# Pre-LN attention and SwiGLU block on one core: another order of the softmax round, one score tile copied out by ACT, a cast moved to GpSimd, and a layer norm moved

## The chip, the core and the metric

One core of a Trainium2 chip runs the whole block in one launch. The metric is the device time in microseconds (us), lower is better. The kernel before ran three times: 1196.97, 1195.42 and 1194.06 us, median 1195.42. Engines are called PE (TensorE; PEld is its weight load), DVE (VectorE), ACT (ScalarE), POOL (GpSimd) and SP (SyncE, which here only issues DMAs).

## The reference

```python
S, D, H, Dh, F = 2048, 448, 16, 28, 1792        # one sequence, float32
n = layernorm(x)                                 # no weights, eps 1e-5
q = (n @ wq)  in 16 heads of 28;  k = n @ wk;  v = n @ wv     # one key/value head for all
p = softmax(q k^T * 28**-0.5);  o = p v
h = x + concat(o) @ wo
m = layernorm(h)
out = h + (silu(m @ w1) * (m @ w3)) @ w2
```

## The kernel before

All operands are split into a high and a low part in a rounded format (`fp32r`), and a product takes three matmuls (high by high, low by high, high by low). There are three parts: a start (layer norm, projections, some score maxima), a long softmax loop, and the feed-forward.

**The work of the loop.** Queries lie in 4 tiles `t` of 512, heads in 4 groups `g` of 4; a pair is a *query group* `i = 4t + g`, 16 in all. The 2048 keys lie in 16 chunks `c` of 128. A *step* is one query group on one key chunk; there are 256. The four heads of a group use four row groups of PE, 32 rows each, side by side. The pieces are:

- **Head** (`H0` to `H3`, class `Head`): three matmuls give 128 keys by 512 queries of one head in a PSUM bank (`pb`, L355); after the third ACT takes the exponential into a `pt`, `xh` or `xl` tile (L362). Of the 32 rows of the query tile `qs`, 28 hold the query; rows 28 and 29 hold minus the row maximum, high and low part, against ones in the keys.
- **Value visit** (`pv1`, function `pv`): four products of the exponentials with the values, in a 128-row mode of PE (`po`, L371, eight instructions). After chunk 15 ACT copies the result to `OT` (L378).
- **Maxima**, which must be there before a group's first head: a *unit* is 128 queries by 512 keys of one head (`pa`, L266). `U` is one matmul and a DVE maximum out of PSUM (L276). `D` and `S` deal with two units: `D` multiplies by a difference of keys (`KD`) and ACT keeps the positive part (`ab`, L287), `S` adds the other product to it and takes the maximum on DVE (L294). The code also has `E`, a unit whose scores ACT copies to SBUF (`kept`), and `R`, the DVE maximum of such a copy later; before, no entry of the order uses them.
- **End of a group's maxima**: when its 64 units are counted, `max_done` reduces them (`nm`, DVE) and splits them (`neg`, POOL, two instructions); 20 entries of the order later (`ROWS = 20`) `max_rows` transposes (`mr`, DVE) and `max_out` issues eight DMAs from SP that write rows 28 and 29 of `qs`. The first head matmul of the group waits for all eight.

**The order.** `EVERY` is a list of entries, written out, that is repeated; one pass is a *round* of four value visits, 48 head matmuls and 16 units. Every engine runs its instructions in this order. PSUM has seven banks for scores: a matmul that starts a bank waits until ACT or DVE has read what stood there. Units run 20 steps (`AHEAD`) ahead of the values. Before, the entries between visits hold 13 or 14 matmuls three times and 24 once; that is the *long visit* below.

**Work hung on steps** (`at(step, ...)`): `build_qs(i)` casts a group's queries to the high part on ACT (L247) and makes the low part on POOL; at the end of tile `t` the output projection `wo_rows` (44 matmuls, L163) runs, then statistics, `ln_rstd` and, for tile 0, `ln_norm` (ACT, L208), the first norm of the feed-forward.

Of the kernel before, what the change touches and what calls it, by code (L numbers as in the profile page):

```python
# [10 lines left out]
AF = mybir.ActivationFunctionType  # L11
# [13 lines left out]
NQ = T // P  # L25
NG = H // 4
NC = S // P
# [8 lines left out]
def block_kernel(  # L36
# [13 lines left out]
    ve, se, ge, pe, sy = nc.vector, nc.scalar, nc.gpsimd, nc.tensor, nc.sync  # L50
# [4 lines left out]
    def f(ap):  # L55
        return ap.bitcast(F32)
# [16 lines left out]
    QR = [keep.tile([P, NG, T], F32, name=f"QR{t}") for t in range(NT)]  # L73
# [10 lines left out]
    def qs_tile():  # L84
        k, n_qs[0] = homes[n_qs[0] % len(homes)], n_qs[0] + 1
        return keep.tile([P, 2, T], F32R, name="qs", tag=f"q{k}")
# [56 lines left out]
    def bank(name="pb"):  # L143
        k = min(free, key=lambda k: order[k])
        free.remove(k)
        ps = ps_w.tile([P, T], F32, name=name, tag=f"bank{k}")
        used[id(ps)] = ps, k
        ready.pop(id(ps), None)
        return ps

    def done(ps, at=None):
        k = used.pop(id(ps))[1]
        order[k] = ready.get(id(ps), clock.end) + 0.7 if at is None else at
        free.append(k)
# [61 lines left out]
    def xt_tiles():  # L216
        return [xt_pool.tile([P, m, T], F32R, name=name) for m, name in ((4, "xh"), (3, "xl"))]

    def ln_tr(t, c, spare=False):
        ps = last = bank()  # L220
        if c == 0:
            XT[t] = xt_tiles()
        xh, xl = XT[t]
        xns = LN[t][3]
        for n in range(NQ):
            pe.transpose(ps[:, n * P : (n + 1) * P], xns[n][:, c * P : (c + 1) * P], ident)  # L226
            clock.mm("full", 0, ps, 0.109, n == 0)
        se.activation(xh[:, c], ps, AF.Copy)
        eng = ve
        if spare:  # L230
            x32 = wk_pool.tile([P, T], F32, name="rb")
            se.activation(x32, ps, AF.Copy)
            eng, ps = ge, x32
        if c < 3:
            eng.tensor_tensor(xl[:, c], ps, f(xh[:, c]), op=ALU.subtract)
        else:
            eng.tensor_tensor(xh[64:128, 3], ps[64:128], f(xh[64:128, 3]), op=ALU.subtract)
        done(last)
# [4 lines left out]
    def build_qs(i, ps=None):  # L243
        t, g = divmod(i, NG)
        q = QS[i] = qs_tile()
        if ps is None:
            se.activation(q[:, 0], QR[t][:, g], AF.Copy)  # L247
            ge.tensor_tensor(q[:, 1], QR[t][:, g], f(q[:, 0]), op=ALU.subtract)
        else:
            se.activation(q[:, 0], ps, AF.Copy)  # L250
            ve.tensor_tensor(q[:, 1], ps, f(q[:, 0]), op=ALU.subtract)
# [205 lines left out]
    with tc.tile_pool(name="start", bufs=1) as sp:  # L457
# [76 lines left out]
        def q(t, g, nb=0):  # L534
            ps = bank()
            mm_D(ps, ps, [w[:, :, 4 * g : 4 * g + 4].rearrange("p c h r -> p c (h r)") for w in WQ],
                 XT[t], slice(0, P), slice(0, T), lambda: pairs(nb))
            if t == g == 0:
                build_qs(0, ps)
            else:  # L540
                se.activation(QR[t][:, g], ps, AF.Copy)
            done(ps)
# [56 lines left out]
        q(0, 1, 0)  # L599
        v0 = kv(0, 1)  # L600
        build_qs(1)
        norm(1, False, 1)
        norm(1, False, 3)
# [105 lines left out]
        q(3, 3, 3)  # L709
        pairs(2)  # L710
        build_qs(2)
        q(2, 1, 0)
        pairs(2)
# [33 lines left out]
    def at(s, fn, *args):  # L747
        todo.setdefault(s, []).append((fn, args))
# [6 lines left out]
    for i in range(NI - 1):  # L755
        e = NC * (i + 1)
# [3 lines left out]
    for t in range(NT - 1):  # L760
        e = NC * NG * (t + 1)


        for n in range(NQ):
            at(e + 14.7, wo_rows, t, n)
            if t == 2:
                at(e + 14.7, lambda c: ln_tr(0, c, True), n)
            late = NC * NG * (t + 2) + 14 if t < 2 else LAST - 12
            at(e + 14.7 if n < NQ - 1 else late + 0.7, ln_stats, t, n)
        at(late + 2, ln_rstd, t)  # L770
    for n in range(NQ):
        at(2 * NC * NG + 25 + 2 * n, ln_norm, 0, n, True)
    for t in range(NT - 1):
        for k in range(2):
            at(NC * NG * (t + 1) + 13 + k, load_w13, 2 * t + k)
# [10 lines left out]
    for s in range(AHEAD, LAST):  # L786
        i, c = divmod(s, NC)
        n, kt = divmod(c, NQ)
# [66 lines left out]
        return True  # L855

    LAG = 1
    EVERY = "U1 U0 pv1 D1 H2 U3 H0 H1 H2 H0 H1 H2 U3 H0 H1 U2 pv1 D0 H1 H3 U2 H3 H3 U2 H2 H1 H1 H2 H2 H0 S1 H3 H0 H1 H0 H3 H1 H3 U2 H1 S0 pv1 U0 H3 H2 H1 H0 H3 H1 H2 H0 H3 H2 U1 H0 U3 pv1 U3 H1 H0 H2 H3 H0 H2 H3 H0 H2 H3".split()

    def tick():  # L860
        for x in later:
            x[0] -= 1
        if later and later[0][0] <= 0:
            i = later.pop(0)[1]
            max_rows(i)
            max_out(i)

    ROWS = 20
    while n_pv[0] + LAG < TAIL:
        for x in EVERY:  # L870
            tick()
# [156 lines left out]
```

## Time and profile before

| | |
|---|---|
| median of three runs | 1195.42 us (1194.06 to 1196.97) |
| the profiled execution's own time | 1193.55 us |
| its span, first to last instruction | 1191.8 us |
| PE / DVE / ACT / POOL busy | 99% / 66% / 61% / 28% |
| first value visit, last value visit | at 92.8 us, at 754.6 us |
| granted PE clock, mean | 1.000 |

The loop is more than half of the span. Inside it DVE and ACT are each busy about nine tenths, in the feed-forward after it they are mostly idle and PE sets the pace. A busy PE in this profile includes matmuls whose ends are modelled, so the loop is read by the distance from one value visit to the next and by what each bank waits for.

### The profile page before, as it was taken

What the parts mean: (1) busy time and instruction counts of PE and PEld (TensorE: products, weight loads), DVE (VectorE), ACT (ScalarE), POOL (GpSimd) and SP (SyncE); (2) the same over time, 40 slices, a digit from 0 to 9 for tenths busy, and PEclk for the clock granted to TensorE, in tenths of its full rate; (3) what the DMA queues carried; (4) which work ended last, traced back from release to release, by engine and by line L of the source; (5) the groups of instructions that cost most, each with busy time, mean ns of one, the idle gap of its engine ahead of it and who ended that gap; (6) DMA issues with size and microseconds to landing.
All of it is one profiled execution on the core that took longest, in us unless ns stands there. A gap on an engine that the chain in (4) does not pass through costs nothing.

```text
span 1191.8 us, 22197 instructions
## 1 busy us (share of the span) xinstructions
PE 1174.8 (99%) x8588; PEld 743.4 (62%) x8588; DVE 786.2 (66%) x1474; ACT 729.6 (61%) x1392; POOL 335.9 (28%) x289
## 2 busy tenths in 40 slices
PE   6999999999999999999999999999999999999998
PEld 4664444445444445444446443688888888888887
DVE  7879899887889988889897981354343334333332
ACT  5739999996999996999997999412111111211111
POOL 5312001101010120011022012354555445455552
PEclk9999999999999999999999999999999999999999
DMA  4000000001000001000001000233000000000000
GB/s 163 10 17 21 19 26 18 19 15 45 19 18 4 19 23 38 19 19 11 10 23 46 10 19 19 57 107 86 1 32 1 1 1 31 1 1 32 1 1 32
DMA packets 36618, 30.72 MB, mean 26 GB/s; under 512 B 13216, under 2 KB 31392, under 8 KB 36512
## 3 DMA queue, kind: packets, MB, share of 16 engines
q1 hardware_dynamic: 36512, 29.30, 8.6%
q8 instruction: 67, 1.10, 0.4%
q14 instruction: 39, 0.32, 0.1%
HBM read 20.37 MB, written 3.80 MB: 20 GB/s over the span
## 4 chain that ended last, share of the span: by engine, by line
PE 93%; DVE 3%; ACT 2%; DMA 0%; SPq 0%; issue 0%; POOLq 0%
PE pa L163 27%; PE po L371 20%; PE pb L355 16%; PE pa L266 14%; PE pb L935 11%; PE pb L163 4%; DVE mx L276 2%; PE pb L226 1%; ACT OT L378 1%; ACT ab L287 1%; DMA X<-in_A_x_dram 0%; ACT pt L362 0%; DVE X L939 0%; DVE xn L210 0%; SPq L174 0%
## 5 line engine op out<-in xcount | busy, mean ns | idle before, releaser
L276 DVE TENSOR_REDUCE mx<-pa 128x1 f32<-128x512 f32 x748 | 481.2, 685 | 62.3 <-PE pa L266 49.2
L355 PE MATMUL pb<-qs,KS 32*128 32x512 f32 x3072 | 393.8, 427 | 0.0
L362 ACT ACTIVATE pt<-pb 128x512 f32<-128x512 f32 x684 | 360.0, 618 | 31.0 <-PE pb L355 15.9
L266 PE MATMUL pa<-KS,qs 32*128 32x512 f32 x886 | 332.2, 460 | 1.9 <-ACT ab L287 0.4
L355 PEld LDWEIGHTS pb<-qs,KS 32*128 32x128 f32 x3072 | 228.6, 182 | 45.6 <-issue 12.6
L163 PE MATMUL pa<-xh,qs 128*128 128x512 f32 x896 | 231.2, 390 | 0.0
L266 PEld LDWEIGHTS pa<-KS,qs 32*128 32x128 f32 x886 | 145.2, 182 | 121.1 <-DVE mx L276 96.5
L163 PEld LDWEIGHTS pa<-xh,qs 128*128 128x128 f32 x896 | 168.1, 188 | 33.7 <-issue 0.8
L371 PE MATMUL po<-pt,VA 128*32 128x512 f32 x1368 | 182.2, 604 | 0.0
L923 DVE TENSOR_TENSOR pt<-pa,pt 128x512 f32<-128x512 f32 x56 | 38.7, 691 | 206.7 <-PE pa L163 202.2
L921 ACT ACTIVATE pt<-pa 128x512 f32<-128x512 f32 x56 | 33.5, 599 | 194.1 <-PE pa L163 194.1
L935 PE MATMUL pb<-w2s,pt 128*128 128x448 f32 x660 | 144.7, 368 | 0.2 <-POOL w2s L444 0.2
L935 PEld LDWEIGHTS pb<-w2s,pt 128*128 128x128 f32 x660 | 123.1, 188 | 13.1 <-POOL w2s L444 0.6
L926 ACT ACTIVATE pt<-pt 128x512 fp32r<-128x512 f32 x56 | 35.5, 633 | 153.4 <-DVE pt L923 149.1
L362 ACT ACTIVATE xh<-pb 128x512 f32<-128x512 f32 x170 | 100.8, 622 | 11.1 <-PE pb L355 9.2
L362 ACT ACTIVATE xl<-pb 128x512 f32<-128x512 f32 x170 | 100.4, 618 | 10.0 <-PE pb L355 6.6
L294 DVE CUSTOM_DVE_ANT_0 ab<-pa,ab 128x512 f32<-128x512 f32 x138 | 93.1, 683 | 7.8 <-ACT ab L287 3.9
L163 PE MATMUL pa<-xl,qs 128*128 128x512 f32 x336 | 94.8, 390 | 0.0
L371 PE MATMUL po<-xl,VA 128*32 128x512 f32 x340 | 89.5, 605 | 0.0
L371 PE MATMUL po<-xh,VA 128*32 128x512 f32 x340 | 89.4, 605 | 0.0
L266 PEld LDWEIGHTS pa<-KD,qs 32*128 32x128 f32 x138 | 23.2, 181 | 99.7 <-ACT pt L362 63.7
L287 ACT ACTIVATE ab<-pa 128x512 f32<-128x512 f32 x138 | 81.6, 602 | 5.4 <-PE pa L266 4.5
(102 smaller groups left out, 1021.2 us busy)
## 6 DMA issues: line engine op xcount, KB each, us to landing
rb<-sd SPq DMA_DIRECT2D x64, 64.0 KB
QR<-OT SPq DMA_DIRECT2D x60, 56.0 KB
QR<-in_B_w_dram SPq DMA_DIRECT2D x16, 192.0 KB
X<-in_A_x_dram SPq DMA_DIRECT2D x3, 896.0 KB
out_dram<-X SPq DMA_DIRECT2D x3, 896.0 KB
qs<-mr SPq DMA_DIRECT2D x128, 2.0 KB
w<-in_B_w_dram SPq DMA_DIRECT2D x8, 192.0 KB
w_wo<-in_B_w_dram SPq DMA_DIRECT2D x6, 224.0 KB
```

The source lines that it names most:

```text
L163: pe.matmul(ps, lhs[b][:, cb, lsl], rhs[a][:, ca, rsl], start=(k == 0), stop=(k == len(terms) - 1),)
L266: pe.matmul(ps, QS[i][r, 0, n * P : (n + 1) * P], KS[0][r, kt * T : (kt + 1) * T] if keys is None else keys[r], start=True, stop=True)
L276: ve.tensor_reduce(self.to(), ps, axis=AX.X, op=ALU.max)
L287: se.activation(self.ab, ps, AF.Relu)
L294: ve.tensor_tensor_reduce(self.ab, ps, self.ab, 1.0, -3.0e38, ALU.add, ALU.max, self.to())
L355: pe.matmul(self.ps, KS[k % 2][r, c * P : (c + 1) * P], QS[i][r, k // 2], start=(k == 0), stop=(k == 2))
L362: se.activation(f(PT[i, c, p][:, jj]), self.ps, AF.Exp, bias=0.0, scale=SCALE)
L371: pe.matmul(PO[i][32 * j : 32 * j + 32], VA[:, c], f(PT[i, c, j // 2][:, j % 2]), start=(c == 0), stop=(c == NC - 1))
L921: se.activation(sg, ps[0], AF.Silu)
L923: ve.tensor_tensor(sg, ps[1], sg, op=ALU.mult)
L926: se.activation(h[:, 0], sg, AF.Copy)
L935: pe.matmul(Y[t][n][:, :D], hid[a][:, n * P : (n + 1) * P], w2s[:, b, :D], start=(k == 0 and m == 0), stop=(k == NF - 1 and m == 2))
```

## The change

1. `EVERY` is another list. It still has four value visits, 48 head matmuls and 16 units, but 11 `U`, two `D` with two `S`, and one unit as `E` (ACT copies it to SBUF) with its maximum `R` on DVE in the next round. The entries between visits are now 13, 24, 15 and 12 matmuls.
2. The cast of the queries is made on POOL instead of ACT for groups 3 to 15.
3. For tile 0 the last statistics, `ln_rstd` and the four `ln_norm` come with the output projection of tile 1 instead of later in the loop, one by one.

`ROWS`, `AHEAD`, and all else stand as before.

```diff
         if ps is None:
-            se.activation(q[:, 0], QR[t][:, g], AF.Copy)
+            if i < 3:
+                se.activation(q[:, 0], QR[t][:, g], AF.Copy)
+            else:
+                ge.tensor_copy(q[:, 0], QR[t][:, g])
             ge.tensor_tensor(q[:, 1], QR[t][:, g], f(q[:, 0]), op=ALU.subtract)
...
+        if t == 1:
+            at(e + 14.7, ln_stats, 0, NQ - 1)
+            at(e + 14.7, ln_rstd, 0)
         for n in range(NQ):
             at(e + 14.7, wo_rows, t, n)
+            if t == 1 and n:
+                for m in ((0, 1), (2,), (3,))[n - 1]:
+                    at(e + 14.7, ln_norm, 0, m, True)
...
-        at(late + 2, ln_rstd, t)
-    for n in range(NQ):
-        at(2 * NC * NG + 25 + 2 * n, ln_norm, 0, n, True)
+        if t:
+            at(late + 2, ln_rstd, t)
...
-    EVERY = "U1 U0 pv1 D1 H2 U3 H0 H1 H2 H0 H1 H2 U3 H0 H1 U2 pv1 D0 H1 H3 U2 H3 H3 U2 H2 H1 H1 H2 H2 H0 S1 H3 H0 H1 H0 H3 H1 H3 U2 H1 S0 pv1 U0 H3 H2 H1 H0 H3 H1 H2 H0 H3 H2 U1 H0 U3 pv1 U3 H1 H0 H2 H3 H0 H2 H3 H0 H2 H3".split()
+    EVERY = "U1 pv1 H3 D0 H1 U2 H3 H0 H1 H3 H0 H1 U2 U3 H0 pv1 D1 H2 S0 H3 H2 U3 H3 H2 H3 H1 H2 H2 H1 H1 U0 H2 H1 H0 H1 H0 U2 H1 H0 U3 pv1 R E3 H0 H2 H1 H0 H3 H2 H1 H3 H2 U0 H3 U2 H0 H1 pv1 H2 H0 S1 H3 H2 U1 H0 H3 H2 H3 H0".split()
```

How the instructions move is shown where a query group's maxima end, on DVE. The place is the end of the maxima of group 2. Before, `nm` and the transpose `mr` stood so (`pa` is a score bank, `ab` the kept positive part; the pairs of ISA are the two instructions of `S`):

```order
L276 TENSOR_REDUCE mx_97<-pa 128x1 x4
L328 TENSOR_REDUCE nm<-mx_97 128x16
L276 TENSOR_REDUCE mx_98<-pa 128x1 x3
L335 STREAM_TRANSPOSE mr<-neg_82 128x32
L276 TENSOR_REDUCE mx_98<-pa 128x1 x4
L294 ISA ab,mx_98<-pa,ab 128x512
L294 ISA mx_98 128x1
L276 TENSOR_REDUCE mx_98<-pa 128x1
```

Now (line numbers are three higher; `kept` is the copy that ACT made):

```order
L279 TENSOR_REDUCE mx_98<-pa 128x1 x4
L310 TENSOR_REDUCE mx_97<-kept 128x1
L331 TENSOR_REDUCE nm<-mx_97 128x16
L279 TENSOR_REDUCE mx_98<-pa 128x1 x2
L297 ISA ab,mx_98<-pa,ab 128x512
L297 ISA mx_98 128x1
L338 STREAM_TRANSPOSE mr<-neg_82 128x32
L279 TENSOR_REDUCE mx_98<-pa 128x1 x5
```

The group's last maximum is now that of the copied unit, `R`, which stands a round behind its `E`: four units of the next group go ahead of it where none did, and the transpose comes behind an `S`. Counted in value visits, `nm` stood five visits and the transpose four visits before the group's first head matmul; now they stand two visits and one visit before it. On PE the same place, with what each instruction waits for, reads now as follows (`po` is a value visit, the `pa` that is first behind it is the product of that `S`, and the last row is the first head matmul of group 2 with its eight DMAs):

```order
L374 MATMUL po<-xh,VA 32x512 x2
L374 MATMUL po<-xl,VA 32x512 x2
L358 MATMUL pb<-qs,KS_85 128x512 [waits Activation_49] x2
L269 MATMUL pa<-KS_85,qs 128x512 [waits DVE_49]
L358 MATMUL pb<-qs,KS_85 128x512 [waits Activation_49]
L358 MATMUL pb<-qs,KS_86 128x512
L269 MATMUL pa<-KS_85,qs 128x512 [waits DVE_49]
L358 MATMUL pb<-qs,KS_86 128x512 x2
L358 MATMUL pb<-qs,KS_85 128x512 x3
L269 MATMUL pa<-KS_85,qs 128x512 [waits Activation_49]
L374 MATMUL po<-pt,VA 32x512 x4
L358 MATMUL pb<-qs,KS_85 128x512 [waits DMAHW4_49,DMAHW3_49,DMAHW5_49,DMAHW2_49,DMAHW6_49,DMAHW1_49,DMAHW7_49,DMAHW0_49,Activation_49]
```

Between the `S` whose maximum precedes the transpose and the matmul that waits for the eight DMAs there is now one value visit. The waiting matmul is the first of its visit.

More of the change, by code (lines that the diff above doesn't have):

```diff
@@ L761, in block_kernel @@
         e = NC * NG * (t + 1)
+        if t == 1:
+            at(e + 14.7, ln_stats, 0, NQ - 1)
+            at(e + 14.7, ln_rstd, 0)
         for n in range(NQ):
             at(e + 14.7, wo_rows, t, n)
+            if t == 1 and n:
+                for m in ((0, 1), (2,), (3,))[n - 1]:
+                    at(e + 14.7, ln_norm, 0, m, True)
             if t == 2:
                 at(e + 14.7, lambda c: ln_tr(0, c, True), n)
+            if t == 0 and n == NQ - 1:
+                continue
             late = NC * NG * (t + 2) + 14 if t < 2 else LAST - 12
             at(e + 14.7 if n < NQ - 1 else late + 0.7, ln_stats, t, n)
-        at(late + 2, ln_rstd, t)
-    for n in range(NQ):
-        at(2 * NC * NG + 25 + 2 * n, ln_norm, 0, n, True)
+        if t:
+            at(late + 2, ln_rstd, t)
     for t in range(NT - 1):
```

## The prediction

> **What bounds the kernel now.** The page's share for PE counts matmuls whose ends are modelled, so I take it only as: no long hole. The change lies in the softmax loop; first the busy times of a stretch inside it (PE, PEld, DVE, ACT, POOL, clock, DMA share, GB/s):
>
> ```profile
> 300.00:400.00 100.00, 99.61 (x956) 46.26 (x952) 89.69 (x167) 94.54 (x185) 12.33 (x14) 1.00 0.07 17
> ```
>
> ACT is the fullest: 185 instructions in 94.54 us, 0.511 us each. The pace is read from the value visits, on PE's timeline:
>
> ```profile
> 313.24 1.06 PE L371 MATMUL po<-pt,VA 128*32 128x512 f32 x8
> ...
> 315.37 1.06 PE L371 MATMUL po<-pt,VA 128*32 128x512 f32 x8
> ...
> 319.63 1.06 PE L371 MATMUL po<-pt,VA 128*32 128x512 f32 x8
> ...
> 323.22 1.07 PE L371 MATMUL po<-pt,VA 128*32 128x512 f32 x8
> ```
>
> A round is 2.13 for the first visit, 4.26 for the next two and 3.59 for the last, 9.98 us. The three short visits stand at what PE needs when its fullest row group has four matmuls. The long one has seven in its fullest row group and is held by something else; its rows, all engines:
>
> ```profile
> 320.62 0.50 PE L266 MATMUL pa<-KD,qs 32*128 32x512 f32 x1
> ...
> 321.16 0.60 ACT L287 ACTIVATE ab<-pa 128x512 f32<-128x512 f32 x1
> 321.65 0.59 ACT L362 ACTIVATE pt<-pb 128x512 f32<-128x512 f32 x1
> ...
> 322.13 0.61 ACT L362 ACTIVATE xh<-pb 128x512 f32<-128x512 f32 x1
> ...
> 322.79 0.50 PE L266 MATMUL pa<-KS,qs 32*128 32x512 f32 x1
> ```
>
> The chain: the first product of the visit (`D`) at 0.99 after the visit's start, ACT's `ab` at 1.53, two exponentials 0.48 apart, the second ends at 322.74, and the last unit of the visit takes its bank 0.05 later; 0.43 behind that the next value visit starts. So the loop is bound by PE's depth in three visits, and by ACT giving back banks in the fourth.
>
> **The change part by part: the round.** PE's depth first. The tail of the loop has visits with three matmuls per row group:
>
> ```profile
> 739.90 1.06 PE L371 MATMUL po<-pt,VA 128*32 128x512 f32 x8
> 740.90 0.97 PE L355 MATMUL pb<-qs,KS 32*128 32x512 f32 x12
> 741.79 0.62 PE L371 MATMUL po<-xh,VA 128*32 128x512 f32 x2
> ```
>
> Depth three takes 1.89, depth four 2.12. Counting the new list by row group, its visits have depths 4, 7, 4, 3 where the old had 4, 4, 4, 7. So one visit can fall by 0.23. The long visit has the same chain: `D1` first, two exponentials, then `U3`, which takes the bank of the second; it keeps 3.59. I walked the round by hand taking a bank as free 0.05 after its release, and 0.48 per ACT step: the depth-three visit comes to 1.93, since a bank arrives 0.04 late, and a four-deep one to 2.13, since its last `U3` waits for an exponential until 1.67. Sum: 3.59 + 2.12 + 1.93 + 2.13 = 9.77.
>
> ACT has the copy more and the cast less. 18 exponentials and `ab` per round become 19; at 0.511 they fill 9.71, and with the copy of `OT` every fourth round (0.62/4) 9.8. So ACT just holds the pace; I take 9.80, a gain of 0.18 in each of 58 rounds: **-10.4**. Bounds: -13.3 (0.23 in full) and 0 (ACT fills the round at 9.98).
>
> **The cast and the norms.** The groups of instructions, with mean ns behind the busy time:
>
> ```profile
> L247 ACT ACTIVATE qs<-QR 128x512 fp32r<-128x512 f32 x15 | 10.9, 727 | 0.0
> ...
> L417 POOL CAST OS<-QR 128x512 fp32r<-128x512 f32 x14 | 8.6, 612 | 37.9 <-DMA QR<-OT 32.1 <-issue 3.8 <-PE pb L355 2.1
> ```
>
> The 13 casts stood in short visits, which stayed at 2.12, so taking 0.73 from ACT there gives nothing by itself; on POOL the nearest row is a cast of 0.61, it stands behind `neg`, not ahead of it, and `qs` is needed some ten visits later. Zero; were POOL late, the next unit would wait, under 1 us, 13 times. The norms stretched two visits, seen beside a common end-of-group visit:
>
> ```profile
> 169.31 1.07 PE L371 MATMUL po<-pt,VA 128*32 128x512 f32 x8
> ```
> ```profile
> 173.29 0.62 PE L371 MATMUL po<-xh,VA 128*32 128x512 f32 x2
> ```
> ```profile
> 510.25 1.06 PE L371 MATMUL po<-pt,VA 128*32 128x512 f32 x8
> 514.71 1.06 PE L371 MATMUL po<-pt,VA 128*32 128x512 f32 x8
> ```
> ```profile
> 466.87 0.60 ACT L362 ACTIVATE xh<-pb 128x512 f32<-128x512 f32 x1 [9.22 <-PE pb L355]
> ```
>
> 4.46 against 3.98 is 0.48; I count the four norms as two such visits, **-0.9**. In their new place ACT idles 9.22 us behind the output projection; four norms fit there, cost nothing, and only if they did not would 3 us come back.
>
> **What the new order adds: a wait for the maxima.** `nm` now follows `R`, and the transpose follows the `S` of the depth-three visit. Before, this was the margin (group 2):
>
> ```profile
> 159.44 0.20 DVE L335 STREAM_TRANSPOSE mr<-neg 128x32 f32<-128x32 f32 x1
> ```
> ```profile
> 160.14 4.66 SPq L343 DMA_DIRECT2D qs<-mr  x8
> ```
> ```profile
> 168.19 0.49 PE L266 MATMUL pa<-KD,qs 32*128 32x512 f32 x1
> ```
>
> From the transpose to the visit with the first head matmul 8.75 us passed, and the eight issues alone take 4.66. The quickest start after a transpose in the trace, and the landing of the same kind of small DMA:
>
> ```profile
> 712.39 0.21 DVE L335 STREAM_TRANSPOSE mr<-neg 128x32 f32<-128x32 f32 x1 [0.60 <-POOL neg L330]
> ```
> ```profile
> 712.67 4.62 SPq L343 DMA_DIRECT2D qs<-mr  x8
> ```
> ```profile
> 755.87 2.46 SPq L385 DMA_DIRECT2D sm<-OT  x4
> ```
> ```profile
> 759.61 0.25 DVE L392 RECIPROCAL sm<-sm 128x16 f32<-128x16 f32 x1 [3.77 <-DMA sm<-OT]
> ```
>
> And the sum of `S` on DVE:
>
> ```profile
> L294 DVE CUSTOM_DVE_ANT_0 ab<-pa,ab 128x512 f32<-128x512 f32 x138 | 93.1, 683 | 7.8 <-ACT ab L287 3.9 <-PE pa L266 3.5
> ```
>
> Four small DMAs were issued by 758.33 and used at 759.61: 1.28 from last issue to use. Now the new order, times from the start of the depth-three visit: the product of `S1` starts at 1.00 and ends at 1.50, DVE takes 0.68 for its sum and a short read, the transpose runs 2.25 to 2.46, the first issue is at 2.53, the last ends at 7.15, the data are there at 8.4. The next visit starts at 1.93, and its first matmul, due at 2.92, is the one that waits. It loses 5.5 us. PE takes its matmuls in order, so everything behind it stands, and ACT and DVE run dry. The wait comes before the first heads of groups 1 to 14 (group 15 has three visits between), also where the output projection stands between, since the transpose is behind that too. **14 x 5.5 = +77.** Bounds: landing with no delay, 4.2 each, +59; the first issue 0.5 late as at 160.14, 6.0 each, +84. I take the landing by the row of the same size.
>
> **The granted clock.** In 5.4 us without a matmul, longer than any in the loop before, the clock can fall. What the trace shows of it is its end and its start:
>
> ```profile
> 1185.71 2.30 PE L935 MATMUL pb<-w2s,pt 128*128 128x448 f32 x10 [0.19 <-POOL w2s L444]
> ```
> ```profile
> 1188.00:1191.00 3.00, 0.01 (x1) 0.00 (x0) 0.67 (x2) 0.00 (x0) 0.00 (x0) 1.00 0.73 269
> 1191.50:1191.80 0.30, 0.00 (x0) 0.00 (x0) 0.00 (x0) 0.00 (x0) 0.00 (x0) 0.50 0.00 0
> ```
> ```profile
> L163 PE MATMUL pb<-xh,OS x4: 395/524/775, 13.0 to 15.9; 128*128 128x512 f32 x4
> ```
>
> The last matmul ended at 1188.01; the clock was full until 1191 and at a half 3.5 us after the end. At the start a matmul took 775 ns at 13.0 and 395 soon after, so a slow stretch lasts some 3.6 us and costs half of it, 1.8. By that one row every wait would end slow, 14 x 1.8 = 25; one sample of the fall is thin, so I take half, **+12**, bounds 0 and 25. [...]
>
> **Sum.** Against the profiled execution: 1193.6 - 10.4 - 0.9 + 77 + 12 = 1271. The median of the runs is 1.9 above that execution, so **1273**.
>
> **The rivals.**
> *Waits without a fall of the clock*: the gap is too short or the phase unlucky. For it: no row shows a fall after a gap inside the kernel. It gives 1261. Chance 0.27.
> *The clock falls each time and ACT gives no gain in the round*: for it the 0.511 per instruction and the 3.5 us row. It gives 1273 + 13 + 10.4 = 1296. Chance 0.12.
> *A shorter wait*: the DMAs overlap more than 4.62 for eight. Against: all starts of eight take 4.6 to 4.7. With half of it, and no fall, 1223. Chance 0.05.
> *Faster*: the maxima arrive in time, and the round's 0.18 stays. This decides at one point: whether the transpose ends 5.9 us (4.62 + 1.28) before the first head matmul is due. Before it did, by far; now it ends 0.46 before. For it stands only that the next group's maxima might run ahead of the heads more than I counted. Then 1195.4 - 11.3 = 1184. Chance 0.06.
>
> **How the numbers follow.** My forecast has 0.50. The range leaves out the faster and the shorter case and the end of the highest: low 1243 (the low bound of the wait and no fall of the clock, 1273 - 18 - 12), high 1296. About 0.2% (2.4 us) is what a measurement can tell from no change; hardly any case ends there. Faster 0.06, same 0.01, slower 0.93.
>
> **What would show it.** In the profile after: PE waiting on a DMA `qs<-mr` 14 times, some 5.5 us each, where before no such row exists; three visits of 2.1 or less and one of 3.6 in a common round; ACT idle for about 5 us at the same places; a granted clock below 1.00 in the loop. Wrong would be: no wait of PE for that DMA, a round of 9.98 or more, or a long visit that is no longer 3.59.

## The result, and the profile after

The changed kernel takes **1291.97 us** (median of four runs, 1289.81 to 1297.66) against 1195.33 for the kernel before (four runs); the ratio is 1.0815, 95% interval 1.0778 to 1.0852. The forecast was 1273, range 1243 to 1296. The profiled execution took 1297.66 us, its span is 1295.9, its mean granted clock 0.956.

From the profile page after: the clock in 40 slices, the chain of what ended last by engine, and the group that now has idle time ahead of it.

```profile
PEclk9999889889889879899899898999999999999999
...
PE 90%; SPq 4%; DMA 3%; DVE 1%; issue 1%; ACT 1%; POOL 0%; POOLq 0%; DVEq 0%; ACTq 0%
...
L358 PE MATMUL pb<-qs,KS 32*128 32x512 f32 x3072 | 403.3, 445 | 79.0 <-DMA qs<-mr 79.0
```

Before, the clock was full in all slices, SP stood at 0% of the chain, and the head matmuls never waited for a DMA. The view of PE's waits gives their count (total, times, longest):

```profile
PE pb L358 <- DMA qs<-mr: 79.0, 14, 6.1
```

One of the 14, on the timeline (the end of the maxima of group 2, the place of the order shown above):

```profile
174.77 0.62 PE L374 MATMUL po<-xh,VA 128*32 128x512 f32 x2
...
176.47 0.69 DVE L297 CUSTOM_DVE_ANT_0 ab<-pa,ab 128x512 f32<-128x512 f32 x1 [0.51 <-PE pa L269]
176.71 1.07 PE L374 MATMUL po<-pt,VA 128*32 128x512 f32 x8
...
177.09 0.21 DVE L338 STREAM_TRANSPOSE mr<-neg 128x32 f32<-128x32 f32 x1
...
177.79 4.65 SPq L346 DMA_DIRECT2D qs<-mr  x8
...
183.81 0.76 PE L358 MATMUL pb<-qs,KS 32*128 32x512 f32 x1 [6.04 <-DMA qs<-mr]
...
184.65 0.60 ACT L290 ACTIVATE ab<-pa 128x512 f32<-128x512 f32 x1 [6.25 <-PE pa L269]
```

Transpose, 0.49 us to the first issue, 4.65 us of issues, 1.37 us from the last issue to the matmul. The matmul itself then takes 0.76 instead of about 0.5: the clock. Stretches around this wait (columns as in the prediction's first row; the clock is the third from the end):

```profile
177.80:182.50 4.70, 0.00 (x0) 0.00 (x0) 0.67 (x2) 0.60 (x2) 1.02 (x1) 1.00 0.02 4
182.50:185.90 3.40, 2.09 (x17) 1.35 (x21) 1.05 (x2) 0.97 (x2) 0.00 (x0) 0.50 0.01 1
185.90:189.30 3.40, 3.40 (x22) 1.45 (x23) 1.66 (x5) 2.39 (x5) 0.00 (x0) 0.50 0.00 0
189.30:192.70 3.40, 3.40 (x37) 1.84 (x34) 3.15 (x5) 3.29 (x7) 0.00 (x0) 0.99 0.03 2
```

PE does nothing for 4.7 us, then the clock is at a half for 6.8 us, of which PE works 5.5. All 14 waits have such a stretch, 109 us of half clock together in the loop.

A common round away from the waits, by its value visits:

```profile
143.14 1.06 PE L374 MATMUL po<-pt,VA 128*32 128x512 f32 x8
145.27 0.62 PE L374 MATMUL po<-xh,VA 128*32 128x512 f32 x2
...
147.21 1.06 PE L374 MATMUL po<-pt,VA 128*32 128x512 f32 x8
149.38 1.07 PE L374 MATMUL po<-pt,VA 128*32 128x512 f32 x8
152.95 0.62 PE L374 MATMUL po<-xh,VA 128*32 128x512 f32 x2
```

2.13, 1.94, 2.17 and 3.57: 9.81 us, against 9.98 before.

To compare loops without the start of the program (the first value visit lies between 92.8 and 96.6 us in the profiles of this case) I use one row per kernel: the copies of a group's result, with the start of the first and of the last. Thirteen groups lie between. Before, then after:

```profile
L378 ACT ACTIVATE OT<-po x14: 616/617/657, 130.5 to 684.7; 128x512 f32<-128x512 f32 x14
```
```profile
L381 ACT ACTIVATE OT<-po x14: 597/597/598, 140.1 to 788.0; 128x512 f32<-128x512 f32 x14
```

554.2 us before, 647.9 after: +93.7 for 13 groups. The row holds 13 of the 14 waits, and the two spans differ by 104.1, so nearly the whole loss is here.

### The profile page after: what moved, and what is told of

Its sections match the earlier page's. It is cut to its first block, busy times and chain, and to the rows that moved or that the text cites. A ratio compares the mean times of both kernels' runs of the same rounds, so it can differ in the third digit from the quotient of the medians.

```text
span 1295.9 us, 22304 instructions
## 1 busy us (share of the span) xinstructions
PE 1200.6 (93%) x8588; PEld 763.7 (59%) x8588; DVE 783.1 (60%) x1474; ACT 754.1 (58%) x1438; POOL 342.3 (26%) x302
## 4 chain that ended last, share of the span: by engine, by line
PE 90%; SPq 4%; DMA 3%; DVE 1%; issue 1%; ACT 1%; POOL 0%; POOLq 0%; DVEq 0%; ACTq 0%
PE pa L163 23%; PE po L374 21%; PE pb L358 21%; PE pa L269 10%; PE pb L945 10%; PE pb L163 4%; SPq L346 4%; DMA qs<-mr 2%; PE pb L226 1%; DMA sd<-sm 0%; DMA X<-in_A_x_dram 0%; DVE xn L210 0%; DVE pt L937 0%; DVE X L949 0%; ACT pt L365 0%
## 5 line engine op out<-in xcount | busy, mean ns | idle before, releaser
L279 DVE TENSOR_REDUCE mx<-pa 128x1 f32<-128x512 f32 x689 | 440.3, 684 | 110.6 <-PE pa L269 90.7
L358 PE MATMUL pb<-qs,KS 32*128 32x512 f32 x3072 | 403.3, 445 | 79.0 <-DMA qs<-mr 79.0
L358 PEld LDWEIGHTS pb<-qs,KS 32*128 32x128 f32 x3072 | 250.6, 196 | 216.4 <-issue 105.8
L365 ACT ACTIVATE pt<-pb 128x512 f32<-128x512 f32 x684 | 364.4, 614 | 17.0 <-PE pb L358 14.0
L269 PEld LDWEIGHTS pa<-KS,qs 32*128 32x128 f32 x886 | 151.0, 194 | 74.3 <-DVE mx L279 52.3
L374 PE MATMUL po<-pt,VA 128*32 128x512 f32 x1368 | 192.4, 636 | 0.4 <-ACT pt L365 0.4
L405 POOL TENSOR_TENSOR OT<-OT,rb 128x512 f32<-128x512 f32 x15 | 19.3, 1284 | 343.2 <-ACT pt L365 125.6
L163 PE MATMUL pa<-xl,qs 128*128 128x512 f32 x336 | 94.8, 390 | 0.0
L374 PE MATMUL po<-xl,VA 128*32 128x512 f32 x340 | 93.8, 631 | 0.0
L374 PE MATMUL po<-xh,VA 128*32 128x512 f32 x340 | 93.8, 631 | 0.0
```

The source lines that it names most:

```text
L163: pe.matmul(ps, lhs[b][:, cb, lsl], rhs[a][:, ca, rsl], start=(k == 0), stop=(k == len(terms) - 1),)
L269: pe.matmul(ps, QS[i][r, 0, n * P : (n + 1) * P], KS[0][r, kt * T : (kt + 1) * T] if keys is None else keys[r], start=True, stop=True)
L279: ve.tensor_reduce(self.to(), ps, axis=AX.X, op=ALU.max)
L358: pe.matmul(self.ps, KS[k % 2][r, c * P : (c + 1) * P], QS[i][r, k // 2], start=(k == 0), stop=(k == 2))
L365: se.activation(f(PT[i, c, p][:, jj]), self.ps, AF.Exp, bias=0.0, scale=SCALE)
L374: pe.matmul(PO[i][32 * j : 32 * j + 32], VA[:, c], f(PT[i, c, j // 2][:, j % 2]), start=(c == 0), stop=(c == NC - 1))
```

## Experiments

Theory: the loss is the wait for the eight DMAs, since the group's last maximum (`R`) stands a round behind its copy, and what the clock loses behind each wait. Rivals: the copy itself overloads ACT; the clock plays no part; the cast or the norms cost or bring something. Times are medians, each ratio is to the kernel before on the same chip with its 95% interval.

**The copy taken out.** In `EVERY`, the copied unit becomes a plain one at the place of `R`:

```diff
-pv1 R E3 H0
+pv1 U3 H0
```

> The changed kernel with the copied unit taken back: its E becomes a plain U at the same place and R is dropped; all else stays. The transpose then stands three value visits before the group's first head matmul. Theory A (the loss is the wait for the maxima, caused by R coming a round late, and the clock that falls in it): no wait of PE for the DMA, clock 1.00, time near 1185 to 1190 (the round's gain of 0.1 to 0.2 us stays). Theory B (the loss is the order itself, ACT and DVE too full in it): the copy off ACT helps by at most 0.5 us in each of 58 rounds, time still over 1250.

1189.98 us, ratio 0.9947 (0.9928 to 0.9966). No wait for `qs<-mr`, clock 1.00.

```profile
L381 ACT ACTIVATE OT<-po x14: 617/620/699, 130.2 to 678.3; 128x512 f32<-128x512 f32 x14
```

548.1 for 13 groups, 6.1 less than before and 99.8 less than after. The loss hangs on that one entry. The rest of the new list brings the gain, nearly all of it: a common round without the copied unit takes 2.12, 2.01, 2.12 and 3.58, that is 9.83 us, against 9.81 with it and 9.98 before.

**`R` earlier.** The copy stays, and `R` goes to the end of the same round:

```diff
-pv1 R E3 H0 ... H2 H3 H0
+pv1 E3 H0 ... H2 H3 H0 R
```

> The changed kernel with R moved to the end of the same round, so the copy stays and its maximum is counted in the round of its E. Transpose three value visits before the first head matmul. Theory A: no wait for the DMA, clock 1.00, round 9.80 as in the changed kernel, time 1184 (1195.4 - 10.4 - 0.9), between 1180 and 1188. Theory B (a round with 19 instructions on ACT is too slow, or the copy itself costs): 1195 or more, and if the order is the loss, over 1250.

1219.29 us, ratio 1.0198 (1.0181 to 1.0215): the view shows no wait for the DMA (two heads stand idle for 0.38 us and start 1.37 and 1.53 us behind the last issue, so these two may be one), the clock is 0.999, yet the time is 35 us over what was expected. A place where a group's maxima end, on the timeline:

```profile
201.79 1.06 PE L374 MATMUL po<-pt,VA 128*32 128x512 f32 x8
...
202.11 0.69 DVE L279 TENSOR_REDUCE mx<-pa 128x1 f32<-128x512 f32 x1
202.71 0.67 DVE L310 TENSOR_REDUCE mx<-kept 128x1 f32<-128x512 f32 x1
...
203.42 0.22 DVE L331 TENSOR_REDUCE nm<-mx 128x16 f32<-128x64 f32 x1
...
204.29 0.50 PE L269 MATMUL pa<-KS,qs 32*128 32x512 f32 x1 [0.33 <-DVE mx L279]
...
204.72 1.06 PE L374 MATMUL po<-pt,VA 128*32 128x512 f32 x8
```

`R` takes DVE for 0.67 us ahead of maxima that must give back a bank; PE waits for that bank. This visit takes 2.93 instead of 2.13, and without `nm` still 2.73, in every round. So `R` has few places: early enough for the DMAs, and not in front of maxima whose banks are wanted. I had counted it as free.

**The wait filled with work.** 23 matmuls whose result nobody reads, ahead of the first head matmul of groups 1 to 14:

```diff
+        if k == 0 and s % NC == 0 and 0 < s < NC * (NI - 1) and s not in filled:
+            filled.add(s)
+            ps = bank("pa")
+            for _ in range(23):
+                pe.matmul(ps, KS[0][:, :P], KS[0][:, :T], start=True, stop=True)
+            done(ps)
         if k == 0:
             heads[j] = Head(*divmod(s, NC), j)
```

> The changed kernel with 23 idle products (128x128 by 512, some 4.9 us, results read by nobody) on PE ahead of the first head matmul of groups 1 to 14, so that PE works while it waits for the maxima. Theory A: the wait's end does not move, but the clock no longer falls; 14 x 2.6 us come back, time near 1256, clock 1.00, the row of PE waiting for the DMA shrinks to under 1 us each. Rival (the clock's fall costs nothing because PE has slack behind the wait): time stays at 1292 within 5 us.

1265.24 us, ratio 1.058 (1.0562 to 1.0598), mean clock 0.997. The same place in the program, one group earlier, and the row of the 13 groups:

```profile
130.14 4.61 SPq L346 DMA_DIRECT2D qs<-mr  x8
...
130.54 5.50 PE L829 MATMUL pa<-KS 128*128 128x512 f32 x23
...
136.10 0.46 PE L358 MATMUL pb<-qs,KS 32*128 32x512 f32 x1
```
```profile
L381 ACT ACTIVATE OT<-po x14: 618/620/632, 138.6 to 757.6; 128x512 f32<-128x512 f32 x14
```

The heads start no earlier, the 5.5 us are lost as before; but the matmul behind takes 0.46 and not 0.76. 619.0 against 647.9: the clock costs 28.9 us in 13 groups, 2.2 per wait, and 26.7 between the medians. The fill adds nothing to the wait: at all 14 places the matmul behind it starts 1.14 to 1.53 us after the last issue, as far as at the same place of the kernel after to 0.05 us. The time is 9 us above the expectation, which had left the clock more of the loss than these 26.7 us.

**The wait made shorter.** The transpose 12 entries behind the maxima instead of 20:

```diff
-    ROWS = 20
+    ROWS = 12
```

> The changed kernel with the transpose 12 instead of 20 entries after the end of the maxima, 1.7 us earlier on DVE. Theory A with a clock that falls only after some 3.5 us without work or more: wait 3.8 us instead of 5.6 and a fall in a few of the 14 waits only, time near 1292 - 14 x 1.75 - 30 = 1238, between 1230 and 1252. Rival (the fall of the clock comes with any wait of this kind): only the shorter wait shows, 1292 - 24 = 1268. Theory B (the wait is not the loss): no change.

1249.16 us, ratio 1.0454 (1.0423 to 1.0485). PE's waits, and two stretches around one of them:

```profile
PE pb L358 <- DMA qs<-mr: 42.1, 11, 4.2
```
```profile
176.37:179.78 3.41, 0.00 (x0) 0.00 (x0) 0.00 (x0) 0.00 (x0) 0.39 (x1) 1.00 0.02 3
179.78:183.19 3.41, 3.32 (x21) 1.45 (x21) 1.98 (x3) 2.17 (x4) 0.00 (x0) 0.50 0.00 0
183.19:186.60 3.41, 3.41 (x32) 1.86 (x32) 2.44 (x5) 2.90 (x7) 0.00 (x0) 1.00 0.02 1
```

3.8 us per wait instead of 5.6, and none behind the three output projections. The clock still fell at all 11 waits (mean 0.969). So the time lies in the expected range, but not for the expected reason, which was that the clock would fall in a few waits only: what went is 36.9 us of waiting and three falls at some 2.1 us each. Here PE worked 3.32 of 3.41 us in the slow stretch, and the next one is fast; in the kernel after it worked 2.09 of 3.40, and the next was slow as well.

**Half of the fill.** The same edit with 11 matmuls. The question was when the clock falls.

```diff
-            for _ in range(23):
+            for _ in range(11):
```

> The changed kernel with 11 idle matmuls (2.6 us) instead of 23 ahead of the first head matmul of groups 1 to 14; nothing waits for their result. [...]

1284.26 us, ratio 1.0744 (1.0703 to 1.0786). The clock fell at 11 of 14 places, with gaps of 2.6 to 3.4 us; its mean is 0.977. Two stretches of 3.41 us with what followed, one without and one with a fall:

```profile
131.92:135.33 3.41, 1.61 (x8) 0.98 (x6) 0.00 (x0) 0.00 (x0) 0.00 (x0) 1.00 0.03 4
135.33:138.74 3.41, 2.44 (x25) 1.22 (x27) 1.83 (x3) 1.90 (x4) 0.00 (x0) 1.00 0.00 1
179.70:183.11 3.41, 1.09 (x13) 0.78 (x13) 0.49 (x1) 0.56 (x2) 0.00 (x0) 1.00 0.01 2
183.11:186.52 3.41, 3.41 (x24) 1.46 (x23) 2.02 (x6) 2.70 (x6) 0.00 (x0) 0.50 0.00 0
```

PE busy 1.61 of 3.41 us (47%): no fall. Busy 1.09 (32%): a fall. The time is 19.0 us above that of the filled kernel (1265.24), so gaps of this length cost the clock as well.

**The copy kept, but not in a group's last round.**

```diff
-                elif kind == "E":
+                elif kind == "E" and u.n < 3:
```

> The changed kernel with its copied unit in three rounds of a group's four; in the last one that unit is reduced straight from PSUM. If the wait comes only from the group's last maximum standing a round behind its copy, there is no wait of PE for qs<-mr, the granted clock stays at 1.0 in the loop, three rounds of four take 9.80 and one 9.83 as without the copy, and the time is 1188 to 1190 us. Rival: a copy on ACT costs by itself (ACT with 19 steps per round): rounds over 9.83 and 1192 us or more.

1187.64 us, ratio 0.9934 (0.9921 to 0.9947). No wait for the DMA.

```profile
L381 ACT ACTIVATE OT<-po x14: 615/623/693, 133.5 to 680.6; 128x512 f32<-128x512 f32 x14
```

547.1 for 13 groups, 100.8 less than after, and 1.0 less than without any copy. The copy is not the cause; its place before a group's end is. Leaving aside the long visit in which ACT copies a result (3.91 to 3.96), three rounds of a group take 9.80 to 9.82; in the fourth DVE has both an `R` and the plain unit, and the depth-three visit takes 2.17 to 2.23 instead of 1.95. That the full DVE is what stretches it was not shown by an experiment.

**Parts 2 and 3 alone**, with the old list:

```diff
-    EVERY = "U1 pv1 H3 D0 H1 U2 ...
+    EVERY = "U1 U0 pv1 D1 H2 U3 ...
```

> The order of before with parts 2 and 3 alone (cast on POOL for groups 3 to 15, norms behind the output projection of tile 1). The prediction's terms: cast 0, norms -0.9, so 1194.5 us (1193.5 to 1195.3) against 1195.4. Rival 1: the cast did hold up ACT, then up to 13 x 0.73 us = 9.5 us less, 1186 us. Rival 2: the cast on POOL comes late or the norms do not fit behind the output projection: 1197 us or more.

1195.71 us, ratio 1.0 (0.999 to 1.0009).

```profile
L381 ACT ACTIVATE OT<-po x14: 615/617/629, 132.7 to 686.2; 128x512 f32<-128x512 f32 x14
```

553.5 against 554.2: 0.7 less in the loop, too little for the runs to show; their median lies 0.4 above the expected range.

**The cast back on ACT**, in the list without the copy:

```diff
-            if i < 3:
+            if i < NI:
```

> The new order without the copy, with the cast of the queries on ACT as before (part 2 undone). If the cast is hidden, as the prediction has it, 1190 us (1189 to 1191) as without this undoing. Rival: in the new order ACT has no room where the cast stands; each of 13 casts then stretches a visit by up to 0.73 us, 1192 to 1199 us.

1190.19 us, ratio 0.9953 (0.994 to 0.9966), as without this edit (1189.98).

```profile
L381 ACT ACTIVATE OT<-po x14: 616/618/693, 135.0 to 683.1; 128x512 f32<-128x512 f32 x14
```

548.1 for 13 groups with the cast on ACT, 548.1 with it on POOL.

**Two issuing engines**, in the kernel after:

```diff
-                sy.dma_start(to[:, :, a], mr[r : r + 16])
+                (sy, se)[k].dma_start(to[:, :, a], mr[r : r + 16])
```

> The changed kernel with the eight DMAs qs<-mr issued from two engines, four from SP and four from ACT. If the wait is the eight issues in a row on SP (4.65 us) plus the landing (1.3 us), it falls by half of the issues, from 5.6 to about 3.3 us, 14 x 2.3 = 32 us, and the clock still falls at most of the 14 places: 1250 to 1262 us. Rival: the transfers themselves set it, whoever issues them: wait 5.6, 1290 us or, with ACT held up by its issues, more.

1276.1 us, ratio 1.0669 (1.0648 to 1.069); 14 to 26 us above the expectation.

```profile
177.18 2.53 ACTq L346 DMA_DIRECT2D qs<-mr  x4
177.21 2.85 SPq L346 DMA_DIRECT2D qs<-mr  x4
179.81 1.57 ACT L365 ACTIVATE pt<-pb 128x512 f32<-128x512 f32 x3 [3.23 <-DMA qs<-mr]
181.66 0.54 PE L358 MATMUL pb<-qs,KS 32*128 32x512 f32 x1 [4.04 <-ACT pt L365]
```

Four issues at a time do shorten the row, but less than by half (2.85 for four, 4.65 for eight), and three exponentials now stand behind ACT's issues and end at 181.38. PE starts at 181.66, 1.60 behind SP's last issue and 0.28 behind ACT, and its row names ACT. The 14 places together speak for the DMAs: PE starts 1.35 to 1.75 behind SP's last issue, at each place 0.2 to 0.3 more than at the same place of the kernel after, while its distance to ACT's last exponential goes from 0.03 to 0.42. The wait fell to 4.0 us, and the clock fell as before (mean 0.960).

**`nm` later.** In the version with the copy kept, `max_done` comes 16 entries later:

```diff
-            max_done(i)
-            later.append([ROWS, i])
+            ended.append([16, i])
```

> The version with the copy in three rounds of four, and nm (with neg behind it) 16 entries later; the transpose keeps its visit. There, the depth-three visit of each group in which nm stands takes 2.17 to 2.23 us and the others 1.95. If it is nm (0.22 us on DVE ahead of a maximum that gives back a bank) that stretches it, that visit falls to 1.95 to 2.0 and the time by 15 x 0.2 = 3 us, to 1184.6 us (1184 to 1186). Rival: something else of a group's end stretches it, or nm stretches another visit as much: 1187 to 1189.

1191.86 us, ratio 0.9975 (0.9961 to 0.9988): slower than without the edit. The last visits of a group, at the end of group 2's maxima:

```profile
161.84 0.20 DVE L338 STREAM_TRANSPOSE mr<-neg 128x32 f32<-128x32 f32 x1
...
162.53 4.65 SPq L346 DMA_DIRECT2D qs<-mr  x8
...
166.67 1.06 PE L374 MATMUL po<-pt,VA 128*32 128x512 f32 x8
...
168.56 0.46 PE L358 MATMUL pb<-qs,KS 32*128 32x512 f32 x1 [0.82 <-ACT pt L365]
...
169.70 1.06 PE L374 MATMUL po<-pt,VA 128*32 128x512 f32 x8
```

The transpose counts its 20 entries from `max_done`, so it moved too, and the wait came back small: this visit takes 3.03 instead of 2.16. The row names ACT, but the matmul starts 1.38 behind the last issue, as in the kernel after (1.37). And the visit that was to get shorter stayed at 2.17 to 2.23, so `nm` was not what stretched it; what does stays open.

**The result copied by DVE**, on top of that, and then without the later `nm`:

```diff
-            if i < NI - 2:
+            if i < 0:
                 se.activation(OT[:, g], PO.pop(i), AF.Copy)
```

> The version with nm later, and the copy of a group's result to OT on DVE for every group instead of ACT. The long visit at a group's end takes 3.95 us against 3.58, and the copy (0.60 on ACT) stands in it. If ACT sets that visit, 14 x 0.37 = 5 us go: about 1180 us (1179 to 1182). Rival: DVE has no room there either, a maximum behind the copy gives its bank back late: 1184 us or more.

1191.62 us, ratio 0.9962 (0.9948 to 0.9977), 11.6 us over the expectation. The group's last long visit fell from 3.92 to 3.67, not to 3.58, the waits that the later `nm` had brought back stayed, and the visit with one of them grew by 1.1 us. From the first to the last value visit the trace is 2.2 us shorter; the medians differ by 0.2.

> The version with the copy in three rounds of four, nm and the transpose where they stand there (not later), and the copy to OT on DVE for every group. In the version with nm later, a group's last long visit fell from 3.92 to 3.67 us by this, and the visit ahead of it stretched to 2.4 to 3.0 us since the maxima came late; that stretch should not be there now. So 13 x 0.25 = 3.3 us less than the version with the copy in three rounds: 1184.4 us (1183 to 1186). Rival: the copy on DVE delays maxima elsewhere by as much: 1187 to 1189 us.

**1184.67 us**, ratio 0.9906 (0.989 to 0.9921): the copy in three rounds of four, `nm` where it was, the result copied by DVE. It is the fastest of all, 3.0 us under the version with the copy kept (which ran on another chip), and 3.2 us shorter in the traces from the first to the last value visit. The long visit at a group's end:

```profile
169.72 1.07 PE L374 MATMUL po<-pt,VA 128*32 128x512 f32 x8
171.01 0.68 DVE L383 COPY OT<-po 128x512 f32<-128x512 f32 x1
173.38 0.62 PE L374 MATMUL po<-xh,VA 128*32 128x512 f32 x2
```

3.66 us here, 3.91 to 3.96 with the copy on ACT.

## Why the prediction was right, step by step

**The round, -10.4.** Right by its visits: 2.13, 1.94, 2.17 and 3.57 against 2.12, 1.93, 2.13 and 3.59 of the walk by hand, 9.81 against 9.77, and the long visit kept its length with another order. The 9.80 that went into the sum came from ACT's fill, and that addition is off: 9.71 with 0.62/4 is 9.87, not 9.8. A common round holds no copy of a result, so its fill is 9.71, below what was measured. That 9.80 fits is luck; that ACT's fill sets the round is not shown. The version with the copy kept, free of the wait, gains 7.1 in 13 groups; with the 0.22 that each group loses in its stretched depth-three visit (13 x 0.22 = 2.9) that is 10.0, and the forecast for 52 rounds and the norms was 52 x 0.18 + 0.9 = 10.3.

**The cast, 0.** Right: 548.1 and 548.1. That was seen in the list without the copy; with cast and copy both on ACT it wasn't tried.

**The norms, -0.9.** Right by the traces, below what the runs can show. In the kernel before two visits were stretched, to 3.96 and 4.46; with parts 2 and 3 alone the same visits take 3.58 and 3.94, and the one with the output projection grows from 11.32 to 11.50, which gives the 0.7. The four norms follow each other behind the output projection:

```profile
522.02 2.72 ACT L208 ACTIVATE xn<-X,nb,rs 128x448 f32<-128x448 f32 x4 [1.60 <-POOL nb L202]
```

**The wait, +77.** Right: 79.0 in 14 waits, 5.64 each for a forecast of 5.5. In the wait shown, one of the longer ones, the issues began 3.02 us after the visit's start instead of 2.53, as the upper bound had it, and the landing took 1.37 for 1.28. That it hangs on `R` alone is shown by the two versions without that `R`, which have no such wait, and by the one with `R` in the round of its copy, which has none above 0.4 us.

**The clock, +12: the mis-sized term.** The row at the end of the program said that every wait ends slow, 25 us, and I took half since one row was thin. The filled kernel puts it at 26.7 (medians) to 31 (14 times 2.2 of the traces). Two things were too low: the fall came at all 14 waits, not at half of them, and a slow stretch lasted 6.8 us at 12 of them (10.2 and 17.1 at the other two), not 3.6. The slow stretch at the start of the program was no measure of one behind a wait: in the wait shown PE worked 2.09 of the first 3.40 slow us, and the next 3.40 were at a half as well. The price also differs between executions: the mean clock was 0.956 in the profiled one and 0.962 to 0.963 in the three others.

**The sum.** With 79 for the wait and 29 for the clock, 1195.4 - 10.4 - 0.9 + 79 + 29 = 1292.1; measured 1291.97. The agreement to 0.1 is luck: for the profiled execution the same sum with 31 for the clock gives 1193.6 - 10.4 - 0.9 + 79 + 31 = 1292 against its own 1297.7. Of the 5 us that are missing, 2.0 lie ahead of the first value visit (94.8 against 92.8); the rest is open. Of the rivals, "waits without a fall of the clock" gave 1261, and that kernel exists: the filled one, at 1265. "The clock falls each time and ACT gives no gain in the round" came near in time (1296) with the wrong mechanism: its second half is refuted by rounds of 9.81. "A shorter wait" and "faster" fell with the 14 waits.

## What to carry to other kernels

In an order written out by hand, follow each result to its farthest consumer before moving it: an entry worth 0.02 us a round (9.81 with it, 9.83 without) cost 7.7 us a group, since the last maximum of a group heads a chain of transpose, eight issues and landing that needs 6.5 us before the first matmul (162.04 to 168.56 above). Price a stall of PE with the clock behind it: here 5.6 us of waiting cost another 1.9 (by the medians) to 2.2 (by the traces). And ask of a delayed step which others count from it: the later `nm` carried the transpose with it.

## What the runs showed of the hardware

- In the trace of the kernel after, the granted clock falls to a half once at each of the 14 waits. In the 3.41 us ahead of the fall PE did nothing in 11 cases and was busy for 1.30 to 1.50 us in three. With 11 matmuls of fill it was busy for 1.09 of 3.41 us ahead of a fall and for 1.61 where none followed. A further fall stands at the loop's start, with PE busy for 3.19 of the 3.41 us before. What sets the fall is not shown. PE's busy time has modelled ends, so the shares are good to some per cent.
- The clock stayed at a half for 6.8 us at 12 of the 14 waits, for 10.2 and 17.1 us at the other two, and for 3.4 us at the loop's start. In the first 3.41 us of the twelve PE was busy for 0 to 2.94 us; with `ROWS = 12`, in the stretch shown above, for 3.32, and there the clock was full behind it. In the stretch of 17.1 us PE was busy for all of the last 10.2 us, so what ends one is not shown either.
- A row that names ACT as releaser can stand for a DMA: in the version with the later `nm`, 8 of the small waits were put down to ACT's `pt` and one to the DMA; they end 1.1 to 1.5 us behind the last issue, as the waits in the kernel after do (1.14 to 1.55), and without the later `nm` none of them is there.
